# Linear attention and a top-1 mixture of experts on one core: decay tables made in place, counts, slots and fetches moved, the last stores deferred

## The chip, the cores and the metric

The kernel runs on one core of a Trainium2 chip. The metric is the device time of one execution in microseconds (us). Matmuls run on TensorE (PE), elementwise work on VectorE (DVE), ScalarE (ACT) and GpSimd (POOL). DMAs are issued from the queues of SyncE (SP), of ACT and of POOL; POOL issues the indirect ones, which gather or scatter rows by an index. Each engine works through its instructions in the order in which they stand, and an instruction that waits holds up all that stand behind it on that engine.

## What is computed

The reference has two parts. The first is linear attention with a decay per head, for 4 batches, 8 heads, 768 positions and 64 features, written here by blocks of 64 positions:

```python
Dmask = np.where(rel >= 0, lam ** rel, 0.0)             # rel = i - j, per head
intra = ((qb @ kb.T) * Dmask) @ vb
inter = (qb * lam ** (pos + 1)) @ kv_state
out[block] = intra + inter
kb_dec = kb * lam ** (block - 1 - pos)
kv_state = lam ** block * kv_state + kb_dec.T @ vb
```

Its output is read as 3072 tokens of 512 features, `x`. The second part sends each token to one of 8 experts:

```python
logits = x @ w_gate + modality_bias[modality_id]
e_idx = argmax(logits)
gate_w = softmax(logits)[e_idx]
h = relu(x[e_idx == e] @ w1[e])                          # w1: 512 x 1024
out[e_idx == e] = gate_w * (h @ w2[e])                   # w2: 1024 x 512
```

## The kernel before

**Attention.** The 24 chunks of 128 positions are worked on in 12 pairs `j`, with one load of 2 MB a pair (`load_half`, L190, three buffers): keys and queries with features in the partitions, values and keys with positions there. For a chunk PE computes scores (L232), DVE multiplies them by the decay table `dk` into `pt` (`masked`, L239), and PE multiplies `pt` by the values (`outputs`, L285) and adds the queries times the state (`from_state`, L278). DVE scales the queries by the table `pq` (`queries`, L222) and the keys by `kdec`, a copy of columns of `dk` (`keys`, L212); PE makes keys times values (`key_values`, L252), and the state is faded on POOL (L265) and added to on DVE (`carried`, L263 and L267). ACT copies the outputs to `xt`, PE turns them into token rows together with the gate's logits (`tokens`, L296), ACT copies these to `xn` (L298) and stores them to the DRAM tensor `xs`.

**The tables.** `lam` is loaded to 8 partitions, its powers are built by seven doublings on DVE (L83) into `tab`, stored to DRAM (`tab_d`, L86) and read back by two DMAs in overlapping rows as `dk` (L90). `pq` comes from PE, by matmuls of the powers with a selecting matrix (`spread_powers`, L109). Until work can begin, PE runs `keep_busy` (L806), matmuls of a tile of zeros.

**Routing.** After the last pair of a batch, `gates`, `route`, `ranks` and `places` (L305 to L382) find for each token its expert and its place among that expert's tokens, and `write_slots` scatters the token's number and weight to `inv` in DRAM (L389, POOL, one indirect DMA for a chunk). `count_tiles` (PE L406, DVE L408 to L413) counts the tokens of each expert up to then. Count "A" is made before the attention ends and gives the two early tiles; count "B" comes from all tokens and gives the list of the others.

**Experts.** A tile has 256 tokens of one expert. The indices of its rows are fetched (SP, L578), the rows gathered into `xg` (POOL, L588), and turned by PE in two parts of four matmuls (`turn_part`, L623), here called T0 and T1. Each fp32 operand is split into a rounded part and a rest (ACT L553, DVE L554), and each product is made of three matmuls (`three`, L636, L639, L640). `wide` makes the first product in four groups, after each of which ACT and DVE make `hh` and `hl` and run a `tail`: it splits a quarter of w2. In the first tile the tails also carry work of the routing of the last batch (`first_tail`): the second one finishes places, the third one writes slots and makes count "B". `second` makes the second product in two halves `t` of 128 tokens, ACT scales it into `y` (L728), and POOL scatters the rows to the output (`store`, L712). The weights of later tiles are fetched by SP.

**The end.** How many tiles there are depends on the data. A fixed number runs always; the rest are nested branches on a count (L1053), none of which is entered in the profiled execution. The second half of the last fixed tile is scaled into a part of `dk`, which is free by then (L725), and its scatter, `store_rest` (L1065), is issued behind the branches.

**Order.** `pinned` chains instructions in the order in which the code makes them, engine by engine; `behind` adds an order, with or without a wait, between two instructions. What is not chained is placed by a scheduler.

Of the kernel before, what the change touches and what calls it, by code (L numbers as in the profile page):

```python
# [6 lines left out]
F32 = mybir.dt.float32  # L7
# [12 lines left out]
HB = 2  # L20
# [20 lines left out]
def linear_attention_moe(tc, qkv, lam, modality, wg, mbias, w1, w2, out):  # L41
    nc = tc.nc
    with ExitStack() as ctx:
# [17 lines left out]
        lam8 = const.tile([H, 1], F32, name="lam8")  # L61
        nc.sync.dma_start(out=lam8, in_=lam)
# [9 lines left out]
        for c in range(HB):  # L72
            for part in (slice(0, 2), slice(2, 4)):
# [3 lines left out]
        tab = const.tile([H, 2 * P], F32, name="tab")  # L77
        nc.vector.memset(tab[:, 0 : P - 1], 0.0)
        nc.vector.memset(tab[:, P - 1 : P], 1.0)
        pw = tab[:, P - 1 :]  # L80
        nc.vector.tensor_copy(out=pw[:, 1:2], in_=lam8)
        for n in (1, 2, 4, 8, 16, 32, 64):
            powers = nc.vector.tensor_scalar(out=pw[:, n + 1 : 2 * n + 1], in0=pw[:, 1 : n + 1],  # L83
                                             scalar1=pw[:, n : n + 1], scalar2=None, op0=ALU.mult)
        tab_d = dram.tile([H, 2 * P], F32, name="tab_d")
        nc.scalar.dma_start(out=tab_d, in_=tab)  # L86

        dk = const.tile([P, 2, NP, P], F32, name="dk")
        for hl in range(2):
            tables = nc.sync.dma_start(  # L90
                out=dk[:, hl],
                in_=bass.AP(tensor=tab_d.tensor, offset=tab_d.offset + hl * 2 * P,
                            ap=[[1, P], [4 * P, NP], [1, P]]),
            )
# [4 lines left out]
        which = const.tile([H, NP, 2, D], F32, name="which")  # L99
        nc.gpsimd.memset(which, 0.0)  # L100
        nc.gpsimd.affine_select(out=which, in_=which, pattern=[[-2, NP], [-1, 2], [0, D]], compare_op=ALU.not_equal,
                                fill=1.0, base=0, channel_multiplier=1)

        pq = const.tile([P, NP, P], F32, name="pq")

        def spread_powers():
            pp = ps.tile([P, NP, P], F32, name="x", bufs=1)
            for p in range(NP):
                nc.tensor.matmul(pp[:, p, :], which[:, p].rearrange("h a d -> h (a d)"), pw[:, 1 : P + 1],  # L109
                                 start=True, stop=True)  # L110
            nc.scalar.copy(out=pq, in_=pp)
# [1003 lines left out]
```

## Time and profile before

| | us |
|---|---|
| median of 3 runs | 417.57 |
| lowest and highest | 417.11, 418.16 |
| the profiled execution | 416.55 |
| its span in the profile | 414.7 |

The granted clock of TensorE was 0.992 over the span. The profile gives, for one execution, the busy time of each engine, what ended each engine's idle time, and a timeline of the instructions. Times within it count from the start of the span. The page shows PE busy in nearly all of the 40 slices of the span; DVE and ACT are idle for a good part, and POOL for most. A matmul of filler counts as busy like any other.

### The profile page before, as it was taken

The numbers are of one execution on the slowest core, as the hardware profiler recorded it, in microseconds if no ns is written. First come the engines' busy times: TensorE is split into PE (matmuls) and PEld (weight loads), VectorE is DVE, ScalarE is ACT, GpSimd is POOL, SyncE is SP. The second block draws the span as 40 slices with busy tenths as digits, with TensorE's granted clock in tenths as the row PEclk, the third lists the DMA queues.
The fourth block names the chain that finished last, engine by engine and source line by source line (L and its number), as shares of the span: only waits on it lengthen the run. The fifth ranks groups of instructions, "written<-read, shape, count | busy, mean of one in ns | idle before, by whom it ended". The sixth has DMA issues, their size and how long they took to land.

```text
span 414.7 us, 9616 instructions
## 1 busy us (share of the span) xinstructions
PE 396.6 (96%) x3864; PEld 353.9 (85%) x3864; DVE 252.1 (61%) x435; ACT 181.2 (44%) x273; POOL 110.0 (27%) x117
## 2 busy tenths in 40 slices
PE   8899999999988999999999999999999999999990
PEld 4599999898886987788989999898989899898980
DVE  5678777879869850667482837466483837375510
ACT  1123323324546331466473726365463827364410
POOL 5010144164156511213031222203040222202000
PEclk9999999999999999999999999999999999999996
DMA  6999999995910176012026584402011111100000
GB/s 210 332 391 381 389 368 337 352 377 216 332 71 3 61 270 242 19 49 81 25 73 235 199 303 143 151 27 80 27 55 51 55 51 38 59 2 28 27 28 19
DMA packets 23347, 63.81 MB, mean 154 GB/s; under 512 B 6901, under 2 KB 8445, under 8 KB 21248
## 3 DMA queue, kind: packets, MB, share of 16 engines
q1 hardware_dynamic: 15056, 43.36, 28.8%
q0 software_dynamic: 4768, 13.08, 9.5%
q10 hardware_dynamic: 3472, 6.69, 4.2%
q8 instruction: 32, 0.52, 0.5%
q14 instruction: 19, 0.16, 0.1%
HBM read 91.40 MB, written 14.07 MB: 254 GB/s over the span
## 4 chain that ended last, share of the span: by engine, by line
PE 42%; issue 29%; DMA 13%; POOL 6%; DVE 3%; another core or an unknown queue 2%; ACT 2%; SPq 1%; POOLq 1%; DVEq 0%; ACTq 0%
DMA out_dram<-y,idx 7%; PE s L232 6%; PE x L296 5%; PE o L285 5%; POOL out_dram L712 4%; PE o L278 3%; DMA idx<-inv 3%; PE s L636 3%; PE s L640 3%; PE s L639 3%; PE o L636 3%; PE o L640 3%; PE o L639 3%; POOL xg L588 2%; PE kv L252 2%
## 5 line engine op out<-in xcount | busy, mean ns | idle before, releaser
L636 PE MATMUL s<-xh,w1h 128*128 128x256 f32 x384 | 108.2, 282 | 1.3 <-DVE hl L654 1.0
L640 PE MATMUL s<-xh,w1l 128*128 128x256 f32 x384 | 107.8, 281 | 0.0
L639 PE MATMUL s<-xl,w1h 128*128 128x256 f32 x384 | 107.8, 281 | 0.0
L654 DVE SCALAR_TENSOR_TENSOR hl<-s,hh 128x512 fp32r<-128x512 f32 x48 | 33.2, 691 | 85.9 <-ACT hh L653 84.2
L636 PE MATMUL o<-w2h,hh 128*128 128x512 f32 x192 | 75.8, 395 | 0.0
L636 PEld LDWEIGHTS s<-xh,w1h 128*128 128x128 f32 x384 | 72.1, 188 | 3.3 <-issue 1.8
L640 PE MATMUL o<-w2h,hl 128*128 128x512 f32 x192 | 74.8, 390 | 0.0
L639 PE MATMUL o<-w2l,hh 128*128 128x512 f32 x192 | 74.8, 389 | 0.0
L640 PEld LDWEIGHTS s<-xh,w1l 128*128 128x128 f32 x384 | 73.5, 191 | 0.0
L639 PEld LDWEIGHTS s<-xl,w1h 128*128 128x128 f32 x384 | 72.2, 188 | 0.4
L554 DVE TENSOR_TENSOR w2l<-raw,w2h 128x1024 fp32r<-128x1024 f32 x48 | 58.8, 1224 | 10.9 <-ACT w2h L553 10.7
L653 ACT ACTIVATE hh<-s 128x512 fp32r<-128x512 f32 x48 | 28.7, 599 | 71.4 <-PE s L640 60.3
L554 DVE TENSOR_TENSOR w1l<-raw,w1h 128x1024 fp32r<-128x1024 f32 x46 | 53.5, 1218 | 4.5 <-ACT yn L700 3.3
L712 POOL DMA_INDIRECT out_dram<-y,idx x19 | 27.4, 1445 | 93.4 <-ACT y L728 93.4
L553 ACT CAST w2h<-raw 128x1024 fp32r<-128x1024 f32 x48 | 49.9, 1039 | 0.0
L588 POOL DMA_INDIRECT xg<-xs,idx x20 | 23.1, 1156 | 85.5 <-PE kv L623 80.9
L553 ACT CAST w1h<-raw 128x1024 fp32r<-128x1024 f32 x46 | 45.2, 1064 | 0.0
L640 PEld LDWEIGHTS o<-w2h,hl 128*128 128x128 f32 x192 | 36.0, 188 | 7.6
L639 PEld LDWEIGHTS o<-w2l,hh 128*128 128x128 f32 x192 | 36.1, 188 | 7.2
L636 PEld LDWEIGHTS o<-w2h,hh 128*128 128x128 f32 x192 | 36.1, 188 | 7.2
L389 POOL DMA_INDIRECT inv<-pay,sloti x24 | 29.5, 1231 | 27.0 <-PE x L296 6.6
L298 ACT COPY xn<-x 128x272 f32<-128x272 f32 x42 | 16.3, 388 | 46.2 <-PE x L296 46.2
(215 smaller groups left out, 470.6 us busy)
## 6 DMA issues: line engine op xcount, KB each, us to landing
raw<-in_w_dram SPq DMA_DIRECT2D x52, 1024.0 KB
load<-in_qkv_dram SPq DMA_DIRECT2D x11, 2048.0 KB
xs<-xn ACTq DMA_DIRECT2D x24, 272.0 KB
load<-in_qkv_dram SPq DMA_DIRECT2D x4, 512.0 KB
w2f<-in_w_dram SPq DMA_DIRECT2D x2, 1024.0 KB
w1h<-in_w_dram SPq DMA_DIRECT2D x2, 1024.0 KB
dk<-tab_d SPq DMA_DIRECT2D x2, 256.0 KB
inv<-pad SPq DMA_DIRECT2D x2, 196.0 KB
```

Of the source, the lines that this page charges most:

```text
L232: pinned(nc.tensor.matmul(sp[:, hl, p, :], kt[r, p, :], qt[r, p, :], start=True, stop=True))
L285: mm = pinned(nc.tensor.matmul(op[blk][halves2[hl ^ blk], p, :], vt[:, (2 * p + hl) * D : (2 * p + hl + 1) * D], pt[:, hl, p, :], start=(g ...
L389: sc = nc.gpsimd.indirect_dma_start(out=inv, out_offset=bass.IndirectOffsetOnAxis(ap=at, axis=0), in_=pay[:, c, :], in_offset=None)
L553: cp = nc.scalar.copy(out=hi, in_=src)
L554: df = nc.vector.tensor_tensor(out=lo, in0=src, in1=hi.bitcast(F32), op=ALU.subtract)
L588: last = nc.gpsimd.indirect_dma_start(out=(to or xg)[t][:m], out_offset=None, in_=xs[:rows, :], in_offset=bass.IndirectOffsetOnAxis(ap=idx ...
L636: mm = pinned(nc.tensor.matmul(out, ah, bh, start=first, stop=False))
L639: pinned(nc.tensor.matmul(out, ah, bl, start=False, stop=False))
L640: return pinned(nc.tensor.matmul(out, al, bh, start=False, stop=last))
L653: act = nc.scalar.activation(out=hh[i], in_=hp, func=AF.Relu)
L654: low = nc.vector.scalar_tensor_tensor(out=hl[i], in0=hp, scalar=0.0, in1=hh[i].bitcast(F32), op0=ALU.max, op1=ALU.subtract)
L712: sc = nc.gpsimd.indirect_dma_start(out=out, out_offset=bass.IndirectOffsetOnAxis(ap=idx[:, t, 0:1], axis=0), in_=y, in_offset=None, bound ...
```

## The change

**Tables.** `lam` is loaded as one row, by ACT's queue. PE multiplies a row of ones by it, which puts the eight decays into each of 128 partitions; DVE copies them, and makes the tables by twelve running products (`tensor_tensor_scan`, 128x128 each): eight for `dk`, each of which starts at the partition's diagonal by a one from `anti`, and four for `pq`. The doublings, `tab_d` and `which` are gone. The filler is 4, 8, 2 and 4 matmuls instead of 16 and 20, with the spreading, scores(0) and scores(1) between.

**Loads.** The quarters of the first load come by part, then by chunk; the second load comes in four pieces with the gate's weights between, the third in two. No load stands behind the tables any more.

**The first two pairs.** Keys and queries are scaled by chunk, the first queries on POOL; the state's first copy is on ACT, and matmuls and DVE work are in another order. Several constants are made by POOL rather than DVE.

**Slots, indices, w2.** At pair `early + 1` one more slot is written, and the index fetches for the early tiles are moved there from the pair behind it. The fetch of w2 waits for the row gather to land; before it waited for a small memset on POOL that stood behind the gather's issue.

**After the attention** the turns T0 and T1 of the first tile stand between the tokens groups of the last chunks, and one `xn` copy of the last chunk goes from DVE to ACT. **Count "B"** goes from the third tail of the first tile to the fourth. **At the end** both halves of the last fixed tile are scaled into `dk`, and `store_rest` issues both scatters.

```diff
+        def spread_decays():
+
+            lp = ps.tile([P, 2, NP], F32, name="x", bufs=1)
+            pinned(nc.tensor.matmul(lp.rearrange("p h a -> p (h a)"), row, lam1, start=True, stop=True))
+            pinned(nc.vector.tensor_copy(out=lamb, in_=lp))
+            for hl in range(2):
+                for p in range(NP):
+                    pinned(nc.vector.tensor_tensor_scan(
+                        out=dk[:, hl, p, :], data0=lamb[:, hl, p : p + 1].to_broadcast([P, P]),
+                        data1=anti, initial=0.0, op0=ALU.mult, op1=ALU.add))
+            for hl, r in enumerate(halves2):
+                pinned(nc.vector.tensor_copy(out=lamp[r], in_=lamb[r, hl]))
+            for p in range(NP):
+                powers.append(pinned(nc.vector.tensor_tensor_scan(
+                    out=pq[:, p, :], data0=lamp[:, p : p + 1].to_broadcast([P, P]),
+                    data1=zero, initial=1.0, op0=ALU.mult, op1=ALU.add)))
...
-        keep_busy(16)
-        sp = scores(0)
-        spread_powers()
-        keep_busy(20)
+        list_constants()
+        keep_busy(4)
+        spread_decays()
+        keep_busy(8)
+        sps = [scores(0)]
+        keep_busy(2)
+        sps.append(scores(1))
+        keep_busy(4)
...
-        pt = masked(0, sp)
-        kds[0] = keys(0)
-        qds[0] = queries(0)
+        pts = [masked(0, sps[0])]
+        kds[0] = keys(0, c0)
+        pts.append(masked(1, sps[1]))
+        qds[0] = queries(0, c1, eng=nc.gpsimd)
...
+            if j == 1:
+                qds[1] = queries(1, c0)
+                pts = [masked(gs[0], sps[0])]
+                kds[1] = keys(1, c0)
+                pts.append(masked(gs[1], sps[1]))
+                queries(1, c1, qds[1])
+                next(turns)
+                next(turns)
+                kp, _ = key_values(gs[:1])
+                carried(gs[0], kp)
+                keys(1, c1, kds[1])
...
+            if j == early + 1:
+                write_slot(mm)
...
-            elif j == early + 2:
+            elif j == early + 1:
                 for i in range(EARLY):
                     fetch_idx(listA, i, idxA[i], after=loads[-1])
+            elif j == early + 2:
                 gathered = fetch_rows(idxA[0], TT, SOON * S, after=fades[-1])
-                asked = nc.gpsimd.memset(flag, 0)
-                behind(asked, gathered, wait=False)
-                fetch_w2(er, {}, asked)
+                fetch_w2(er, {}, gathered)
         turns = turned(pairs - 1)
+        next(turns)
+        rows0 = turn_part(0, TT, pin=True)
+        next(turns)
+        split(*rows0)
+        rows1 = turn_part(1, TT, pin=True)
+        split(*rows1)
         next(turns)
         next(turns)
         gated(pairs - 2)
-        rows0 = turn_part(0, TT, pin=True)
-        split(*rows0)
-        rows1 = turn_part(1, TT, pin=True)
-        next(turns)
-        split(*rows1)
-        next(turns)
...
             elif i == 2:
                 write_slots(next(begun[1]), begun[0])
+            else:
                 begun.append(count_tiles(XT + 1, "B"))
...
-                if kept is not None and t == 1:
-                    nc.scalar.activation(out=kept, in_=yp, func=AF.Copy, scale=weight)
-                    return lambda: store(kept, 1)
+                if kept is not None:
+                    nc.scalar.activation(out=kept[t], in_=yp, func=AF.Copy, scale=weight)
+                    continue
...
+            return lambda: [store(kept[t], t) for t in range(2)]
...
-        kept = dk[:, 0].rearrange("p a t -> p (a t)")
+        kept = [dk[:, t].rearrange("p a t -> p (a t)") for t in range(2)]
```

Three places show what this makes of the order of instructions. DVE at the start, before, from the doublings on (x2 means twice in a row):

```order
L83 TENSOR_SCALAR tab<-tab 8x16
L83 TENSOR_SCALAR tab<-tab 8x32
L83 TENSOR_SCALAR tab<-tab 8x64
L410 TENSOR_SCALAR geA<-thr 1x96
L410 TENSOR_SCALAR geB<-thr 1x96
L239 TENSOR_TENSOR pt<-s,dk 128x512 x2
L212 TENSOR_TENSOR kd<-load,kdec 128x1024
L222 TENSOR_TENSOR qd<-load,pq 128x512
L263 COPY state_117<-kv 128x256
L239 TENSOR_TENSOR pt<-s,dk 128x1024
L212 TENSOR_TENSOR kd<-load,kdec 128x1024
L222 TENSOR_TENSOR qd<-load,pq 128x1024
```

And after; the running products are shown under the name of their kind, at L85 and L91:

```order
L151 MEMSET onesb 128x128
L82 COPY lamb<-x 128x8
L85 SCALAR_TENSOR_TENSOR dk<-lamb,anti 128x128 x8
L89 COPY lamp<-lamb 64x4 x2
L91 SCALAR_TENSOR_TENSOR pq<-lamp,zero 128x128 x4
L242 TENSOR_TENSOR pt<-s,dk 128x512 x2
L213 TENSOR_TENSOR kd<-load,kdec 128x512
L242 TENSOR_TENSOR pt<-s,dk 128x1024
L213 TENSOR_TENSOR kd<-load,kdec 128x512
L270 TENSOR_TENSOR state_108<-faded,kv 128x256
L225 TENSOR_TENSOR qd<-load,pq 128x512
L242 TENSOR_TENSOR pt<-s,dk 128x1024
```

The two operations on `geA` and `geB` and the doublings are gone from there, twelve running products stand ahead of the first `pt`, and a half `kd`, the second `pt` and the other half follow, where the whole `kd` and a `qd` stood.

PE around count "B" in the first tile, before, between the third and the fourth group of the first product (`s`):

```order
L636 MATMUL s<-xh_135,w1h 128x256
L639 MATMUL s<-xl_137,w1h 128x256
L640 MATMUL s<-xh_135,w1l 128x256
L406 LDWEIGHTS onesb
L406 MATMUL kv<-ohsum,onesb 128x8
L636 MATMUL s<-xh_134,w1h 128x256
L639 MATMUL s<-xl_136,w1h 128x256
L640 MATMUL s<-xh_134,w1l 128x256
```

And after, at the end of the fourth group:

```order
L639 MATMUL s<-xh_121,w1h 128x256
L642 MATMUL s<-xl_123,w1h 128x256
L643 MATMUL s<-xh_121,w1l 128x256
L409 LDWEIGHTS onesb
L409 MATMUL kv<-ohsum,onesb 128x8
L626 MATMUL x<-ident,xg_116 128x128
L626 MATMUL x<-ident,xg_117 128x128
L626 MATMUL x<-ident,xg_116 128x128
L626 MATMUL x<-ident,xg_117 128x128
L639 MATMUL o<-w2h,hh_1802 128x512
L642 MATMUL o<-w2l,hh_1802 128x512
L643 MATMUL o<-w2h,hl_1804 128x512
```

The count's matmul now stands one group of 24 matmuls later, right ahead of T0 (the turns into `x`); T1 (the turns into `kv`) comes behind the first twelve matmuls of the second product, where it stood right behind T0.

POOL ahead of the first branch, before:

```order
L588 DMA xg_126<-xs,idx_4397 128x544
L588 DMA xg_127<-xs,idx_4397 128x544
L712 DMA out_dram<-y,idx_3927 3072x512 x2
L712 DMA out_dram<-y,idx_4162 3072x512 x2
L712 DMA out_dram<-y,idx_4397 3072x512
L1053 COMPARE_AND_BRANCH
L588 DMA xg_126<-xs,idx_4923 128x544
```

The same after:

```order
L591 DMA xg_116<-xs,idx_4386 128x544
L591 DMA xg_117<-xs,idx_4386 128x544
L715 DMA out_dram<-y,idx_3916 3072x512 x2
L715 DMA out_dram<-y,idx_4151 3072x512 x2
L715 DMA out_dram<-dk,idx_4386 3072x512
L1078 COMPARE_AND_BRANCH
L591 DMA xg_116<-xs,idx_4908 128x544
```

And after, the end of POOL's instructions:

```order
L1078 UNCONDITIONAL_BRANCH
L1078 ISA
L1078 UNCONDITIONAL_BRANCH
L715 DMA out_dram<-dk,idx_4386 3072x512
L1136 UNCONDITIONAL_BRANCH
L1136 ISA
```

One scatter from `y` became one from `dk` in the same place ahead of the branch, and one scatter from `dk` stands behind the branches, as one did before.

## Rows read from the trace of the kernel before

**Rows 1.** The page, busy time of TensorE: us, share of the span, instructions.

```profile
PE 396.6 (96%) x3864; PEld 353.9 (85%) x3864; DVE 252.1 (61%) x435; ACT 181.2 (44%) x273; POOL 110.0 (27%) x117
```

**Rows 2.** Waits of PE: engine, line, waited for: us, times, longest.

```profile
PE kv L623 <- DVE cntB L408: 2.0, 1, 2.0
PE kv L252 <- DVE kd L212: 1.8, 1, 1.8
...
PE kv L406 <- DVE ohsum L376: 1.0, 1, 1.0
```

**Rows 3.** Timeline of PE, 0 to 31: start, us, engine, line, operation [idle before].

```profile
1.28 5.55 PE L806 MATMUL o<-busy 128*128 128x512 bf16 x16 [1.28 <-DVE busy L76]
...
9.91 3.63 PE L806 MATMUL o<-busy 128*128 128x512 bf16 x16
15.38 0.69 PE L252 MATMUL kv<-load,kd 128*64 128x64 f32 x16 [1.84 <-DVE kd L212]
...
17.09 1.09 PE L285 MATMUL o<-pt,load 128*64 128x128 f32 x16
...
28.79 2.06 PE L232 MATMUL s<-load 64*128 64x128 f32 x32
```

**Rows 4.** Timeline of DVE, 0 to 16.

```profile
3.02 0.08 DVE L81 COPY tab<-lam 8x1 f32<-8x1 f32 x1
...
6.08 1.07 DVE L410 TENSOR_SCALAR geA<-thr 1x96 f32<-1x96 f32 x1 [0.35 <-POOL thr L789]
...
12.83 1.36 DVE L239 TENSOR_TENSOR pt<-s,dk 128x512 f32<-128x512 f32 x2 [5.63 <-DMA dk<-tab_d]
14.11 1.22 DVE L212 TENSOR_TENSOR kd<-load,kdec 128x1024 f32<-128x1024 f32 x1
15.24 0.68 DVE L222 TENSOR_TENSOR qd<-load,pq 128x512 f32<-128x512 f32 x1
```

**Rows 5.** DVE groups by shape, 0 to 60: busy us, mean ns of one.

```profile
L267 DVE TENSOR_TENSOR state<-faded,kv 128x256 f32<-128x256 f32 x8 | 3.4, 421 | 5.6 <-POOL faded L265 2.9 <-PE kv L252 2.6
L222 DVE TENSOR_TENSOR qd<-load,pq 128x512 f32<-128x512 f32 x3 | 2.1, 684 | 0.0
```

**Rows 6.** POOL groups by shape, 0 to 30.

```profile
L265 POOL TENSOR_TENSOR faded<-state,pq 128x256 f32<-128x256 f32 x4 | 2.5, 623 | 16.6 <-DVE state L267 10.5 <-DVE state L263 6.1
L139 POOL COPY iw<-ident 64x256 f32<-64x256 f32 x4 | 1.6, 396 | 0.2
L137 POOL MEMSET iw<- 128x544 f32 x2 | 1.2, 593 | 0.0
```

**Rows 7.** Stretches: us, busy of PE, PEld, DVE, ACT, POOL, PEclk, DMA share, GB/s.

```profile
3.00:5.00 2.00, 2.00 (x6) 0.71 (x5) 1.63 (x15) 0.00 (x0) 0.00 (x0) 1.00 1.03 360
...
9.00:10.00 1.00, 1.00 (x9) 0.88 (x9) 0.00 (x0) 0.00 (x0) 0.93 (x5) 1.00 0.02 5
10.00:13.00 3.00, 3.00 (x15) 1.35 (x15) 0.17 (x1) 0.59 (x1) 0.55 (x3) 1.00 0.80 193
...
20.00:28.00 8.00, 8.00 (x184) 7.64 (x179) 6.22 (x8) 2.86 (x7) 1.25 (x2) 1.00 1.02 411
```

**Rows 8.** Timeline of DVE, 118 to 130.

```profile
120.39 0.17 DVE L376 TENSOR_TENSOR ohsum<-ohsum,ohn 128x8 bf16<-128x8 bf16 x1
123.33 0.69 DVE L654 SCALAR_TENSOR_TENSOR hl<-s,hh 128x512 fp32r<-128x512 f32 x1 [2.78 <-ACT hh L653]
...
125.96 0.11 DVE L408 COPY cntB<-kv 1x8 f32<-1x8 f32 x1
126.10 0.24 DVE L411 TENSOR_TENSOR geB<-cntB,geB 1x96 f32<-1x96 f32 x1
```

**Rows 9.** Timeline of ACT, 118 to 130.

```profile
122.70 0.60 ACT L653 ACTIVATE hh<-s 128x512 fp32r<-128x512 f32 x1 [4.38 <-remote]
```

**Rows 10.** Timeline of POOL, 380 to 415.

```profile
406.59 0.98 POOL L712 DMA_INDIRECT out_dram<-dk,idx  x1 [5.34 <-DMA out_dram<-y,idx]
```

**Rows 11.** Timeline of ACT, 398 to 415.

```profile
404.69 0.69 ACT L725 ACTIVATE dk<-o,idx 128x512 f32<-128x512 f32 x1 [4.70 <-PE o L640]
```

More of the change, by code (lines that the diff above doesn't have):

```diff
@@ L58, in behind, with pinned @@
             tc.add_manual_dep(later.ins, first.ins.name, info, reason="order")
-        lam8 = const.tile([H, 1], F32, name="lam8")
-        nc.sync.dma_start(out=lam8, in_=lam)
+        halves2 = [slice(hl * D, (hl + 1) * D) for hl in range(2)]
+        pins = {}
+        def pinned(op):
+            if op.ins.engine in pins:
+                behind(op, pins[op.ins.engine], wait=False)
+            pins[op.ins.engine] = op
+            return op
+        lam1 = const.tile([1, H], F32, name="lam1")
+        nc.scalar.dma_start(out=lam1, in_=lam)
+        row = const.tile([1, P], F32, name="row")
+        nc.vector.memset(row, 1.0)
+        lamb = const.tile([P, 2, NP], F32, name="lamb")
+        lamp = const.tile([P, NP], F32, name="lamp")
+        def spread_decays():
[13 more added lines that the diff above has]
+                    data1=zero, initial=1.0, op0=ALU.mult, op1=ALU.add)))
         def load_tile():
@@ L71, in linear_attention_moe @@
         first = load_tile()
-        for c in range(HB):
-            for part in (slice(0, 2), slice(2, 4)):
+        for part in (slice(0, 2), slice(2, 4)):
+            for c in range(HB):
                 nc.sync.dma_start(out=first[:, part, c], in_=source(0)[:, part, c])
@@ L76, in linear_attention_moe @@
         nc.vector.memset(busy, 0.0)
[L77 to L86, printed above, removed]
-        dk = const.tile([P, 2, NP, P], F32, name="dk")
[L89 to L94, printed above, removed]
+        zero = const.tile([P, P], F32, name="zero")
+        nc.vector.memset(zero, 0.0)
+        anti = const.tile([P, P], F32, name="anti")
+        nc.gpsimd.affine_select(out=anti, in_=zero, pattern=[[1, P]], compare_op=ALU.not_equal,
+                                fill=1.0, base=1 - P, channel_multiplier=1)
+        dk = const.tile([P, 2, NP, P], F32, name="dk")
+        pq = const.tile([P, NP, P], F32, name="pq")
+        powers = []
         ident = const.tile([P, P], F32, name="ident")
@@ L98, in linear_attention_moe @@
         wgt = const.tile([P, HB, NP, E], F32, name="wgt")
[L99 to L111, printed above, removed]
         def later(op):
-            behind(op, powers)
+            behind(op, powers[-1])
             return op
@@ L189, in load_half @@
             t = load_tile()
-            ld = nc.sync.dma_start(out=t, in_=source(g))
-            behind(ld, tables, wait=False)
+            whole = slice(0, HB)
+            for part in (slice(0, 2), slice(2, 4)) if g < LOADS else (slice(0, 4),):
+                for c in (slice(i, i + 1) for i in range(HB)) if g == 1 else (whole,):
+                    ld = nc.sync.dma_start(out=t[:, part, c], in_=source(g)[:, part, c])
+                    if g == 1 and part.start == c.start == 0:
+                        nc.sync.dma_start(out=wgt, in_=wg)
             loads.append(ld)
@@ L262, in carried @@
             if c == 0:
-                return pinned(nc.vector.tensor_copy(out=new, in_=kp[:, g % HB]))
+                return pinned(copy(out=new, in_=kp[:, g % HB]))
             faded = work.tile([P, NP, D], F32, name="faded", bufs=1)
@@ L601, in fetch_regs, with fetch_halves @@
             return er, {"cond": cr}
-        def fetch_halves(to, src, er, kw, after):
+        def fetch_halves(to, src, er, kw, after, wait):
             n = src.shape[2] // 2
```

141 lines of the change are left out of this document (69 added, 72 removed).

## Prediction

> **What bounds the kernel now.** I read the page's busy times first. TensorE (PE) is busy in 396.6 us of the 414.7 us span [rows 1], so time can be won in two ways alone: by taking out waits of PE, or by letting it reach its first useful matmul sooner. The list of PE's waits [rows 2] has three that this change could touch: 2.0 us before the second half of a turn (L623), which waits for VectorE's (DVE's) copy of a count, 1.8 us at the start before the first key-value products, and 1.0 us before the count's matmul (L406).
>
> PE's own rows at the start [rows 3] say more than its waits. From 1.28 to 13.54 us it does filler (L806 on a tile of zeros: 16 in the first row, 16 in the last), one scores group and the spreading of the powers; only at 15.38 does kv (L252) begin, and from there PE works without a pause to the scores at 28.79. The filler counts as busy, so the loss is not the 1.8 us of the list but most of 15 us. DVE's rows [rows 4] name what it waits for: lam's copy starts at 3.02, the powers are built and sent to DRAM and back, and the masked scores start at 12.83 after 5.63 us idle, ended by the table's DMA. Then pt takes 1.28 us to the start of kd at 14.11, and kd ends at 15.33, 0.05 before kv.
>
> **The start, A.** Tables no longer go through DRAM: PE spreads the eight decays, DVE copies them and makes twelve running products of 128x128, and pt, half of kd and kv follow. lam now comes by the ACT queue; I keep its time, 3.0. The small matmul and DVE's copy bring the first product to about 3.6. The trace before has no such running product, so I bound one by other DVE rows [rows 5]: 128x256 takes 0.421 and 128x512 takes 0.684, which is 0.158 plus 1.03 ns a column, and a follower starts some 0.09 before the end shown (kd to qd in [rows 4]: 14.11 + 1.22 against 15.24). For 128 columns at that rate the spacing is 0.20. Since every product needs the one before it, I take two column times for an element, 0.42 less 0.09, or 0.33; as a high bound 0.50, three column times. So the tables are done at 3.6 + 12 x 0.33 + 0.3 for the two small copies = 7.9 (6.3 to 9.9). Add 1.28 for pt and 0.69 for one half of kd: kv at K = 9.9.
>
> [...]
>
> PE itself can't be there much sooner: from 1.28, four fillers, the spreading, eight, scores(0), two, scores(1), four. With 0.35 for one of the early fillers (5.55 / 16), 0.23 for a late one (3.63 / 16) and 1.03 for each scores group (2.06 / 2) [rows 3], that is 1.28 + 12 x 0.35 + 0.2 + 1.03 + 0.5 + 1.03 + 0.9 = 9.1. So faster products can bring up to 0.8 more. The first loads are ahead of this: at 360 GB/s [rows 7], 2 MB take about 5.8 us, and the quarter that kd needs is the third.
>
> From kv on, before takes 13.41 us to the scores at 28.79. After has 1.0 less, since scores(1) stands ahead of kv, but DVE becomes the bound once: from_state(1) needs the second state of the pair, behind pt(2), pt(3), one half of kd and two of qd. PE reaches kv(1)'s end at K + 4.2 (kv 0.6, outputs, from_state, outputs 1.0 each [rows 3], kv 0.6); DVE then does a state, two halves of kd or qd before pt(3), two pt, one half after and the state: 2 x 0.42 + 3 x 0.6 + 2 x 1.13 = 4.9, plus a 0.4 wait for the first scores: K + 9.6. PE wants it at about K + 8.7. With 0.4 for two tokens groups in a row that share one PSUM tile, the scores come at K + 12.4 + 1.4 = K + 13.8 to 14.1. I take K + 14.1 = 24.0, so A gains **4.8**.
>
> Does it last? Between 9 and 10 us DMA moves 5 GB/s and from 10 to 13 it moves small pieces of the table at less than half of the later rate [rows 7]; without them the loads begin about 5 us sooner. So loads and PE shift by nearly the same amount, and I let the gain hold. The qd that goes to POOL, 128x512, is hidden: twice the 0.62 of a 128x256 there [rows 6], from the tables' end to about 9.2, and PE wants it 1.7 after K.
>
> **The early tiles, B.** The 1.0 us at L406 goes wholly: the count now stands behind the last wide group, 24 matmuls later, and ohsum was ready at 120.56 [rows 8]. The 2.0 us wait hides a queue on DVE: hl at 123.33 came late because ACT's hh began at 122.70 after 4.38 us idle [rows 9], and the count's copy stood behind it, w2l and three small operations, at 125.96 [rows 8]. After, T0 and twelve matmuls of the second product (12 x 0.23 = 2.7 us) stand between the count and T1, but the copy stands behind hl and w2l of the last quarter too (0.69 [rows 8] and, as other operations of 128x1024, 1.22 [rows 4]). I expect 0.0 to 1.3 us of it to remain and take 0.4, so 1.6 is won. Of the turns that are now spread between the last tokens groups I count nothing: one xn copy goes to ACT, which is busy with casts there. B gains 1.0 + 1.6 = **2.6**, between 1.0 and 3.0. The list that follows the count starts behind the same w1l casts as before, so nothing later moves.
>
> **Slots, index fetches and w2.** The added write_slot and the index fetch one pair sooner lie on POOL and SP while PE works; w2's fetch now waits for the landing of the row gather rather than its issue. SP has no load queued behind it, and w2 is not used until the first second product. Counted at 0, up to 1 us lost if it lands late.
>
> **The tail, D.** POOL's last scatter starts at 406.59 although ACT's tile was ready at 404.69 + 0.69 = 405.38 [rows 10, 11]: its idle time ended on the landing of the scatter before it, for which the branch's bookkeeping on POOL waits. With both scatters behind the branches that bookkeeping would be over long before, and the last scatter would start 1.1 us sooner. But the order of the changed program has one scatter of dk ahead of the first branch and one behind, as before. I follow the order: **0**.
>
> **Sum.** 4.8 + 2.6 + 0 = 7.4. The profiled execution took 416.55 (414.7 of span, 1.85 around it) and would take 409.2; it lies 1.0 under the median, 417.57, so the forecast is 417.57 - 7.4 = **410.2**.
>
> **Rivals.** (1) The scatters do go behind the branches, as the change says: 409.1. For it, the source; against it, the order. (2) T1 still waits for the count and the start is as forecast: gain 4.8 + 1.0, 411.8. For it, ACT's late hh [rows 9]. (3) The products are slowed by POOL, which builds iw and the list constants at the same time. Before, a DVE operation of 1x96 took 1.07 at 6.08 [rows 4], where one of that shape takes 0.24 later [rows 8]; POOL filled iw and the list constants then. Three POOL copies of 0.4 [rows 6] beside the products make the tables 1.2 later: A is 3.6, the time 411.4. [...] (4) Slower: a running product costs an element what the slow 1x96 row cost, 11 ns [rows 4], so 1.43 each. Tables at 3.6 + 17.2 + 0.3 = 21.1, K at 23.1, scores at 37.2, 8.4 lost against 2.6 won: 423.4. It decides from 0.95 us each on, where A loses what B wins. Against it, the rows of full tiles cost 1.3 to 1.6 ns a column [rows 5].
>
> **How the numbers follow.** Forecast 0.52, (1) 0.10, (2) 0.13, (3) 0.14, (4) 0.04; 0.07 for smaller losses that add up (A at 2, B at 1: 414.6). The range leaves out (4) and the worst of the last: 407.8 (A 5.6, B 3.0, D 1.1) to 413.6. A difference within 0.3% (1.25 us) can't be told from none. Faster by more 0.93, within 0.03, slower 0.04.
>
> **What would show it.** A: dk's products end near 7.9 and kv starts near 9.9; a spacing of 0.2 or 0.5 is read at once from DVE's rows, and a new PE wait of about 1 us before the second half of from_state(1). B: no wait at L409, and under 1.3 before T1. D: POOL's last scatter again about 1.2 us after ACT's tile. I am wrong if PE reaches the scores of the third pair later than 26, or if a gain there is back by 100 us as waits for loads.

## The result, and the profile after

The changed kernel took 413.2 us in the median (412.57 to 416.87, 12 runs) against 418.32 for the kernel before in the same comparison (414.77 to 421.35, 12 runs): a ratio of 0.9893, with a 95% interval of 0.9860 to 0.9926. On the 417.57 us that the prediction starts from that is a gain of 4.5 us (3.1 to 5.8 by the interval), where 7.4 was forecast; 413.1 lies inside the range, 0.5 from its slow end. The profiled execution's span is 411.2 us where before had 414.7. Some executions of a kernel are slower as a whole; the ratios leave these out and are not made from the medians, so they need not be the quotients of the medians beside them.

TensorE's waits in the changed kernel (engine, line, what it waited for: us, times, longest):

```profile
PE o L815 <- DVE busy L107: 1.4, 1, 1.4
PE x L299 <- ACT xn L301: 1.1, 2, 0.6
PE s L639 <- DVE hl L657: 0.8, 1, 0.8
PE kv L255 <- DVE kd L213: 0.7, 1, 0.7
PE o L281 <- DVE state L270: 0.5, 1, 0.5
```

The two waits of 2.0 and 1.0 us around the count [rows 2] are gone, and the start's 1.8 is 0.7. A wait for `hl` in the third expert tile is left as it was, 0.8 at 174 us here and 1.0 at 180 us before:

```profile
PE s L636 <- DVE hl L654: 1.0, 1, 1.0
```

TensorE's rows at the start (start, us, operation, idle before it):

```profile
10.67 0.69 PE L255 MATMUL kv<-load,kd 128*64 128x64 f32 x16 [0.74 <-DVE kd L213]
...
17.82 0.68 PE L299 MATMUL x<-iw,xt 128*64 128x136 f32 x8 [0.49 <-ACT xn L301]
...
19.82 1.09 PE L281 MATMUL o<-qd,state 64*64 64x128 f32 x28 [0.48 <-DVE state L270]
...
24.60 2.06 PE L235 MATMUL s<-load 64*128 64x128 f32 x32
```

`kv` begins at 10.67 instead of 15.38 and the scores of the third pair at 24.60 instead of 28.79 [rows 3], 4.19 us sooner. VectorE's rows of the same stretch, where the tables are made:

```profile
3.86 0.17 DVE L82 COPY lamb<-x 128x8 f32<-128x8 f32 x1 [0.48 <-PE x L81]
4.13 2.94 DVE L85 TENSOR_TENSOR_SCAN dk<-lamb,anti 128x128 f32<-128x128 f32 x8
6.99 0.31 DVE L89 COPY lamp<-lamb 64x4 f32<-64x4 f32 x2
7.34 1.37 DVE L91 TENSOR_TENSOR_SCAN pq<-lamp,zero 128x128 f32<-128x128 f32 x4
8.63 1.26 DVE L242 TENSOR_TENSOR pt<-s,dk 128x512 f32<-128x512 f32 x2
9.81 0.81 DVE L213 TENSOR_TENSOR kd<-load,kdec 128x512 f32<-128x512 f32 x1
```

Eight running products take 2.94 us, 0.367 each in the mean, and four take 1.37, 0.34 each. The loads no longer stop for the table [rows 7] (stretch: busy of PE, PEld, DVE, ACT, POOL, clock, DMA share, GB/s):

```profile
9.00:10.00 1.00, 0.88 (x3) 0.20 (x3) 1.00 (x3) 0.00 (x0) 1.00 (x1) 1.00 1.04 366
10.00:13.00 3.00, 2.33 (x48) 2.16 (x48) 2.35 (x3) 0.96 (x2) 2.54 (x7) 1.00 1.05 389
```

Behind the attention VectorE copies the count (L411) at 122.02 in the changed kernel, and no row of TensorE waits for it:

```profile
116.89 0.17 DVE L379 TENSOR_TENSOR ohsum<-ohsum,ohn 128x8 bf16<-128x8 bf16 x1
...
122.02 0.15 DVE L411 COPY cntB<-kv 1x8 f32<-1x8 f32 x1
```

So far all is near the forecast. Set side by side, the two profiled executions show where the gain stood: the changed kernel is ahead by 4.19 us at the third pair's scores, by 3.41 at the first matmul of the first expert tile (110.64 and 107.23), by 6.53 at that of the second tile (137.55 and 131.02), and by 3.89 at the last tile's second product (393.61 and 389.72). **2.64 us are lost over eleven tiles in which TensorE waits in neither kernel but for that one `hl` of the third, 1.0 before and 0.8 after.** One first product of each, from its first matmul to the turn behind its 96th, is enough to see it. Before (the start is the first number):

```profile
220.57 0.28 PE L636 MATMUL s<-xh,w1h 128*128 128x256 f32 x1
...
231.88 0.60 PE L623 MATMUL x<-ident,xg 128*128 128x128 f32 x4
```

After:

```profile
215.01 0.28 PE L639 MATMUL s<-xh,w1h 128*128 128x256 f32 x1
...
226.54 0.60 PE L626 MATMUL x<-ident,xg 128*128 128x128 f32 x4
```

11.31 us before, 11.53 after, for the same 96 matmuls of the same shape at a full clock (1.00 granted): 0.1178 and 0.1201 us apart, 0.22 a tile, 2.4 of the 2.64 in eleven tiles; most of the rest is in the third tile. The matmuls of the second product are 0.227 apart in both.

### The profile page after: what moved, and what is told of

The parts are those of the page before. It is cut to its first block, busy times and chain, and to the rows that moved or that the text cites. A ratio compares the mean times of both kernels' runs of the same rounds, so it can differ in the third digit from the quotient of the medians.

```text
span 411.2 us, 9569 instructions
## 1 busy us (share of the span) xinstructions
PE 395.3 (96%) x3839; PEld 354.5 (86%) x3840; DVE 252.4 (61%) x438; ACT 181.6 (44%) x274; POOL 113.6 (28%) x119
## 4 chain that ended last, share of the span: by engine, by line
PE 61%; issue 21%; DMA 7%; POOL 5%; DVE 3%; another core or an unknown queue 1%; ACT 1%; POOLq 1%; DVEq 0%; ACTq 0%
DMA out_dram<-y,idx 7%; PE s L639 6%; PE s L642 6%; PE s L643 6%; PE o L288 5%; PE o L639 5%; PE o L643 5%; PE o L642 5%; PE x L299 5%; PE s L235 5%; PE o L281 3%; POOL out_dram L715 3%; PE kv L255 2%; POOL xg L591 2%; PE s L674 1%
## 5 line engine op out<-in xcount | busy, mean ns | idle before, releaser
L591 POOL DMA_INDIRECT xg<-xs,idx x20 | 24.0, 1202 | 87.0 <-PE kv L626 82.8
L715 POOL DMA_INDIRECT out_dram<-y,idx x18 | 26.2, 1457 | 78.1 <-ACT y L731 74.7
L392 POOL DMA_INDIRECT inv<-pay,sloti x24 | 28.5, 1189 | 22.3 <-PE x L299 8.1
```

The source lines that it names most:

```text
L392: sc = nc.gpsimd.indirect_dma_start(out=inv, out_offset=bass.IndirectOffsetOnAxis(ap=at, axis=0), in_=pay[:, c, :], in_offset=None)
L591: last = nc.gpsimd.indirect_dma_start(out=(to or xg)[t][:m], out_offset=None, in_=xs[:rows, :], in_offset=bass.IndirectOffsetOnAxis(ap=idx ...
L715: sc = nc.gpsimd.indirect_dma_start(out=out, out_offset=bass.IndirectOffsetOnAxis(ap=idx[:, t, 0:1], axis=0), in_=y, in_offset=None, bound ...
```

## The experiments

Each ratio is against runs of the kernel before on the same chip, which differ from chip to chip by some 7 us (medians of 413.3 to 420.6); I compare the times of one chip with each other. "Changed kernel" is after, "a32" is the changed kernel with the edit of the first experiment.

### What makes the same matmuls slower: the place in SBUF

The diff does not touch the first product. What it changes for it is where the tiles lie: other constants are placed ahead of them. `strip` is a small constant that is placed between the tokens `xh`, `xl` and the weights `w1h`, `w1l`; a wider `strip` moves the weights and all behind it, not the tokens. `row` is placed ahead of both. The first four kernels, on one chip (before 414.0 us), are the changed kernel again, two that move its tiles, and before with the move of a32:

```diff
 a32: the changed kernel, weights 32 bytes further
-        strip = const.tile([P, 2], F32, name="strip")
+        strip = const.tile([P, 16], F32, name="strip")
 a64: the changed kernel, tokens and weights 64 bytes further
-        row = const.tile([1, P], F32, name="row")
+        row = const.tile([1, P + 16], F32, name="row")[:, :P]
 b32: the kernel before, weights 32 bytes further
-        strip = const.tile([P, 2], F32, name="strip")
+        strip = const.tile([P, 16], F32, name="strip")
```

> The changed kernel once more, beside the others on one chip. Every theory: span near 411.2, time 1.1% below before; matmuls of the first product of a tile 0.1201 us apart.

> The changed kernel with one small constant tile (strip) made 32 bytes wider a partition, so that all that lies behind it, w1h and w1l among it, starts at a multiple of 64 bytes as before; no instruction differs. Theory 1 (the first product runs slower since its weights lie 32 bytes past a multiple of 64): the spacing falls from 0.1201 to 0.1178, 0.21 us a tile, 2.3 to 2.7 us in all, span 408.5 to 408.9. Theory 2 (xh and xl, 64 bytes past a multiple of 128, are to blame) and theory 3 (it is not the place in memory but what runs beside it): 411.2 as the changed kernel.

> The changed kernel with an early constant tile (row) made 64 bytes wider, so that xh and xl start at a multiple of 128 as before, and w1h and w1l stay 32 bytes past a multiple of 64; no instruction differs. Theory 2: spacing 0.1178, span near 408.7. Theories 1 and 3: 0.1201 and 411.2.

> The kernel before with strip 32 bytes wider, so that w1h and w1l lie 32 bytes past a multiple of 64; xh and xl stay where they were; no instruction differs. Theory 1: it loses what the changed kernel lost, spacing 0.1201, 2.3 to 2.7 us, span 417.0 to 417.4. Theories 2 and 3: 414.7 as before.

The changed kernel again took 410.56 us (ratio 0.9919 [0.9889, 0.9949]), a32 408.04 (0.9851 [0.9818, 0.9884]), a64 410.54 (0.9909 [0.9875, 0.9942]), b32 416.46 (1.0059 [1.0032, 1.0086]). 32 bytes in a constant that has nothing to do with the product bring 2.5 us, and the first product of a32 is back at 11.31 us. Moving both operands alike brings nothing, so it is not the place of one that counts. The wider `strip` makes the kernel before slower: the sign depends on where one starts. None of the three theories on record holds as it stands: theory 1 wanted 0.1201 us between the matmuls of b32, which has 0.1187; a64 speaks against theory 2 and a32 against theory 3. b32's 2.5 us are more than its first products explain (11.39 for 11.31, 1.0 us in twelve tiles); the rest stays open.

Two larger moves have one run each, and the third and fourth run repeat a move beside a32 (before 413.32 us):

```diff
 a_s64: the changed kernel, weights 64 bytes further
+        strip = const.tile([P, 24], F32, name="strip")
 b96: the kernel before, weights 96 bytes further
+        strip = const.tile([P, 32], F32, name="strip")
```

> The changed kernel with strip 64 bytes wider: w1h and w1l still lie 32 bytes past a multiple of 64, but 64 bytes further from xh. Counted modulo 128, w1h less xh was 32 in the two kernels with the full loss (0.1201 us apart, 0.21 us a tile) and 96 in the one of before with shifted weights (0.1187, 0.09 a tile). If that distance sets the size: 0.1187 here. If the program does, or the weights' place alone: 0.1201 as in the changed kernel.

> The kernel before with strip 96 bytes wider: w1h and w1l lie 32 bytes past a multiple of 64, and w1h less xh is 32 modulo 128. If the distance sets the size of the loss: 0.1201 and 0.21 us a tile. If the program does: 0.1187 and 0.09 a tile as with strip 32 bytes wider.

> The changed kernel with strip 64 bytes wider, timed beside a32 on one chip. In its first trace the matmuls of the first product stood 0.1167 us apart, closer than in the kernel before (0.1178). If that holds: 1152 x 1.1 ns = 1.3 us below a32. If it was that execution's: as a32 or above.

> a32 as the yardstick: 1.3 to 1.5% below before, spacing 0.1178.

a_s64 took 410.82 us and b96 421.03 beside a single 417.12 of before; a_s64_again 407.83 (0.9849 [0.9805, 0.9893]), a32_third 407.87 (0.9854 [0.9810, 0.9898]). A first product takes 11.21 us in a_s64, the least of all, and 11.52 in b96. The distance modulo 128 had given b96 rightly and a_s64 wrongly (0.1187 expected, 0.1168 measured). What orders them is the distance from the tokens to the weights modulo 256 bytes, which I found only after these seven placements. The last run was to forecast an eighth: before with 160 bytes more has the distance 224 of a_s64.

```diff
 b160: the kernel before, weights 160 bytes further
+        strip = const.tile([P, 48], F32, name="strip")
```

> The kernel before with its small tile strip made 48 columns wide, so that everything placed behind it in SBUF, the first product's weights among it, lies 160 bytes further while the tokens stay. Theory (the distance from the tokens to the weights, taken modulo 256, sets the spacing of the first product's matmuls): the distance goes from 64 to 224, which was the fastest with the changed kernel; the matmuls start 0.1167 us apart where before has 0.1178, 0.11 us less per tile of 96, about 1.2 us less over the program. Rival (each shift of the weights of before costs, as 32 bytes did with 0.1187 and 96 bytes with 0.1201): 0.120 or more, the program some 2.5 us longer than before.

Its first product:

```profile
198.79 0.28 PE L636 MATMUL s<-xh,w1h 128*128 128x256 f32 x1
...
210.00 0.60 PE L623 MATMUL x<-ident,xg 128*128 128x128 f32 x4
```

11.21 us, as a_s64 has, to the hundredth; the rival's 11.5 is out. The time was 418.36 us against 420.55 on that chip (0.9972 [0.9936, 1.0009]), which agrees with the 1.2 us forecast and can't by itself be told from none. All eight (bytes within a partition, from the compiled programs):

| kernel | weights at | tokens at | distance mod 256 | one first product, us |
|---|---|---|---|---|
| before | 146496 | 81408 | 64 | 11.31 |
| b32 | 146528 | 81408 | 96 | 11.39 |
| b96 | 146592 | 81408 | 160 | 11.52 |
| b160 | 146656 | 81408 | 224 | 11.21 |
| changed | 145376 | 79936 | 160 | 11.53 |
| a32 | 145408 | 79936 | 192 | 11.31 |
| a_s64 | 145440 | 79936 | 224 | 11.21 |
| a64 | 145440 | 80000 | 160 | 11.52 |

a64 and a_s64 have their weights in one place and differ by 0.31 us; changed and a_s64 share the tokens' place and differ by 0.32. The other twelve traces, at distances of 64, 160, 192 and 224, have the same times to 0.01. That the distance sets it is inferred from these eight, of which one was forecast. All that lies behind `strip` moves with the weights, so that it is the weights and not another tile there is argued, from what the product reads; why the distance matters is not shown. The times follow less exactly than the traces: a_s64_again should be 1.2 us below a32_third and is 0.04 below, with a wait of 1.0 for a row gather in its profiled execution.

### What the start is worth

a32scan2 is a32 with the four products of `pq` made twice, so that `kv` begins later and nothing else changes. a32order is a32 with the order that the kernel before has for the first two pairs, tables and loads as changed. Since a32order was on another chip, a32 was run again beside it, and a64order is the same edit on a_s64.

```diff
 a32scan2
+            for p in range(NP):
+                powers.append(pinned(nc.vector.tensor_tensor_scan(
+                    out=pq[:, p, :], data0=lamp[:, p : p + 1].to_broadcast([P, P]),
+                    data1=zero, initial=1.0, op0=ALU.mult, op1=ALU.add)))
 a32order
-        pts = [masked(0, sps[0])]
-        kds[0] = keys(0, c0)
-        pts.append(masked(1, sps[1]))
-        qds[0] = queries(0, c1, eng=nc.gpsimd)
+        pt = masked(0, sp)
+        kds[0] = keys(0)
+        qds[0] = queries(0)
...
-            if j == 1:
-                qds[1] = queries(1, c0)
-                pts = [masked(gs[0], sps[0])]
-                kds[1] = keys(1, c0)
...
+            pts = [masked(g, sp) for g, sp in zip(gs, sps)]
```

> a32 with the four running products of pq made twice, 1.37 us more of DVE's work ahead of pt. If the chain of products sets the start (A as forecast): kv 1.3 later, at 12.0, and the time 1.2 to 1.4 us above a32, so near 409.3. Rival, the loads set the pace after the first pairs and the start has slack: within 0.4 us of a32.

> a32 with the work of the first two pairs in the order of the kernel before (whole kd, first qd and state on DVE, scores(1) behind kv, one more filler), tables and loads as changed. If the tables are what A is worth: kv at 11.2 rather than 10.7, no waits at tokens and from_state(1) (0.5 each in a32), the scores of the third pair within 0.3 us of a32's 24.6 and the time within 0.4 us. If the order by chunk carries a part of A: scores of the third pair at 25.5 or later and 0.8 to 1.5 us above a32.

> a32 once more, as the yardstick of the three kernels beside it. If its gain is the forecast's A and B without the loss to the place of the weights: 1.3 to 1.8% below before.

> a_s64 with the first two pairs in the order of the kernel before (as a32order, which took a32's time): within 0.3 us of a_s64, 0.1167 apart.

a32scan2's scores of the third pair come at 25.88, 1.28 later than 24.60, and its time is 411.97 us (0.9865 [0.9807, 0.9923]); the nearest kernel on that chip, a32tact below, took 410.73. So a delay of the start comes out at the end, 1.24 of 1.28 if a32tact stands for a32, though an interval of 2 us to each side does not prove the size. The two traces say the same: what is 1.28 later at the third pair is 1.12 later at the first matmul of the last tile (377.15 and 376.03). a32order took 408.3 us (0.9870 [0.9839, 0.9901]), a32_again 408.27 (0.9868 [0.9836, 0.9899]), a64order 407.57 (0.9865 [0.9806, 0.9923]) beside 407.83 of a_s64_again. TensorE's rows of a32order:

```profile
11.11 0.69 PE L255 MATMUL kv<-load,kd 128*64 128x64 f32 x16 [1.65 <-DVE kd L213]
...
24.52 2.06 PE L235 MATMUL s<-load 64*128 64x128 f32 x32
```

`kv` begins 0.44 later and the third pair no later: the whole of the start comes from tables and loads, which no run separates, and the work by chunk in the first pairs is worth nothing.

### The count

```diff
 bcnt: the kernel before, count "B" in the fourth tail
             elif i == 2:
                 write_slots(next(begun[1]), begun[0])
+            else:
                 begun.append(count_tiles(XT + 1, "B"))
 a32cnt: a32, count "B" back in the third tail
-            else:
```

> The kernel before with one part of the change alone: count B in the fourth tail of the first tile instead of the third; memory as before. As forecast for B: 1.0 us at the count's matmul and 1.6 before T1, time 2.6 us or 0.6% below before. If the wait before T1 is not there in most executions: 0.7 to 1.0 us, 0.2%. Rival, the count's copy behind hl and w2l makes T1 wait in its place: no gain.

> a32 with count B back in the third tail. As forecast for B: 1.0 us at the count's matmul and up to 2.0 before T1 come back, time 1.0 to 3.0 us above a32. Rival, the count was hidden in most executions: within 0.4 us of a32.

bcnt took 417.22 us beside 419.17 of before, 0.9989 [0.9951, 1.0027]: not to be told from none. Both waits at the count are gone from its trace, and a new one stands in the first product of the second tile:

```profile
PE s L636 <- DVE hl L654: 1.9, 2, 1.0
```

Before has 1.0 there in one wait, bcnt 1.9 in two: near 1 us of the 3 is given back. The changed kernel has no such wait in its second tile. a32cnt took 409.52 (0.9894 [0.9863, 0.9926]), 1.25 more than a32_again on its chip:

```profile
PE kv L409 <- DVE ohsum L379: 0.7, 1, 0.7
```

The wait of 0.7 at the count's matmul is back; that before T1 is not. T1's wait is no fixed price in the kernel before either: 2.0, 2.1, 2.0 and 1.3 us in the profiled executions of before, b_again, b160 and b96, and none in that of b32. Where it is 2.0 or 2.1, ACT's `hh` comes late, behind an idle time that ends on something the profile does not name (`remote`), as in [rows 9]; here in b_again, with 4.43 in b160 and no such row in b32:

```profile
126.81 0.60 ACT L653 ACTIVATE hh<-s 128x512 fp32r<-128x512 f32 x1 [4.39 <-remote]
```

It seems to go by the chip. The nine traces that have the wait for `hl` in the third tile, of 0.7 to 1.0, come from the first comparison and from chips where before takes 417 to 421 us, and T1's wait is in all four of them that count in the third tail. The other eleven, b32 and a32cnt among them, are from chips where before takes 413.3 to 414.4, and have neither. What ACT waits for stays open.

### The slot

a32slot is a32 without the additional `write_slot` at pair `early + 1`.

```diff
-            if j == early + 1:
-                write_slot(mm)
```

> a32 without the one added slot write at pair early + 1 (it moves into the next slot's place, all slots are still written). If that write costs PE a wait at 80 to 86 us (0.5 to 0.6 in the changed kernel, after ACT's xn or a state): the wait is gone, 0.4 to 0.6 us below a32. If the wait comes from elsewhere: within 0.3 us of a32, or up to 0.5 above where the index fetch then waits for the slots.

It took 409.2 us (0.9889 [0.9848, 0.9931]), 0.9 more than a32_again; the intervals overlap. The wait of 0.5 near 81 us that it was to remove is still there, and its trace has a wait that a32 has not: T0 waits for the gathered rows.

```profile
PE x L626 <- DMA xg<-xs,idxA: 0.5, 1, 0.5
```

a_s64_again, which writes the additional slot, waits there too, for 1.0, so that this wait comes from the slot is not shown.

### The tail

The changed order has one of the two scatters of `dk` ahead of the first branch. a32tact lets the first wait for ACT's last scaling, so that both stand behind the branches.

```diff
+            def rest():
+                first = store(kept[0], 0)
+                behind(first, scaled[1], wait=True)
+                store(kept[1], 1)
```

> a32 with the scatter of the first half made to wait for ACT's last scaling, by which both scatters come to stand behind the branches. If the branch's bookkeeping behind the early scatter sets the last one's start: it is off the path, but two scatters must now be issued from 0.2 us after ACT's end, 1.27 apart, so the last starts 1.4 to 1.5 after ACT's end where it was 1.5 in the changed kernel: time within 0.3 us of a32. If scatters close behind each other also land later: 0.3 to 1 us above a32.

It took 410.73 us (0.9819 [0.9766, 0.9873]). POOL's last rows, and ACT's last scaling:

```profile
399.42 0.98 POOL L715 DMA_INDIRECT out_dram<-dk,idx  x1 [21.19 <-ACTq L1085]
400.70 0.99 POOL L715 DMA_INDIRECT out_dram<-dk,idx  x1 [0.30 <-issue]
```

```profile
398.46 0.69 ACT L730 ACTIVATE dk<-o,idx 128x512 f32<-128x512 f32 x1 [4.75 <-PE o L643]
```

The last scatter starts 1.55 us after ACT's end (399.15 to 400.70). In the changed kernel, where it waits for the scatter before it, it is 1.54 (401.54 to 403.08), in a32 1.40, and 1.33 to 1.95 over the thirteen traces of that order:

```profile
396.37 0.98 POOL L715 DMA_INDIRECT out_dram<-dk,idx  x1 [15.98 <-ACT dk L728]
403.08 0.98 POOL L715 DMA_INDIRECT out_dram<-dk,idx  x1 [5.72 <-DMA out_dram<-y,idx]
```

```profile
400.85 0.69 ACT L728 ACTIVATE dk<-o,idx 128x512 f32<-128x512 f32 x1 [4.75 <-PE o L643]
```

No a32 was timed beside a32tact, so what its time gained is not shown. In its trace the wait on the early scatter's landing is only traded for the scatter ahead, 1.28 long. A first scatter behind the branches that does not wait for the last scaling was not tried.

### The kernel before, once more

Before varies by 4 to 7 us between executions on one chip, the changed kernel by 2 to 4. A second trace of it shows one possible reason:

> The kernel before once more, for a second trace of it. If the 2.0 us wait ahead of T1 in the first trace belongs to the program, it is here again. If it comes from one late release (ACT's hh began 3.1 us after its matmuls had ended there), it is gone or shorter here, and B was worth 1.0 us rather than 2.6 in most executions.

It took 420.68 us. The table's second DMA landed late there, and VectorE's second `pt` waited for it; the wait for `kd` is 3.2 us instead of 1.8, and behind it TensorE's granted clock, the third number from the end in the stretches, is half:

```profile
15.10 0.69 DVE L239 TENSOR_TENSOR pt<-s,dk 128x512 f32<-128x512 f32 x1 [0.74 <-DMA dk<-tab_d]
```

```profile
PE kv L252 <- DVE kd L212: 3.2, 1, 3.2
```

```profile
16.00:18.00 2.00, 1.02 (x16) 0.93 (x16) 1.53 (x2) 0.00 (x0) 0.00 (x0) 0.50 1.01 418
18.00:20.00 2.00, 2.00 (x18) 1.79 (x16) 0.42 (x1) 0.00 (x0) 0.62 (x1) 0.50 1.04 317
20.00:22.00 2.00, 2.00 (x20) 1.63 (x18) 1.84 (x2) 0.00 (x0) 0.00 (x0) 0.50 0.92 365
22.00:24.00 2.00, 2.00 (x30) 1.83 (x30) 1.06 (x2) 0.58 (x1) 0.00 (x0) 0.81 1.00 406
```

Ahead of `kv`, which runs at 0.50 and takes 1.12 us where it took 0.69 [rows 3], TensorE had no matmul for 3.22 us; in the first trace the pause there is 1.84 us and the clock behind it stays at 1.00 (16 to 20 us). That the longer pause halves the clock is not shown by this one trace. The scores of the third pair come at 32.99, 4.2 after those of [rows 3]. None of the fourteen traces with the new tables has such a stretch. How often it happened in the timed runs is not shown, but their mean granted clocks point that way: it is 0.983 in b_again, at most 0.985 in 13 of the 111 timed executions of before and its variants in these experiments, this one among them, and at least 0.986 in all 68 of the changed kernel and its variants.

## Why the prediction was right or wrong

**The start, A: right, a little too large.** 4.8 was forecast, and the third pair's scores came 4.2 sooner, at 24.60 for 24.0. The first product began at 4.13 instead of 3.6, twelve of them took 4.3 us instead of 4.0, so `kv` came at 10.67 for 9.9; from there 13.93 us for 14.1. The two pauses that I foresaw as 0.4, a guess that no row gives, and about 1 were 0.49 and 0.48. That a running product takes two column times, 0.33, was my estimate, which no row of the kernel before shows; it held: they start 0.36 and 0.32 apart, against the 0.20 that [rows 5] give for 128 columns of the operations there. The price of rival 4 (1.43 each) is out. The high bound of 0.50, called three column times, is 0.46 by the rows that it names; it did not matter.

**Does it last? Mostly.** The lead of the changed kernel stays at 4.2 to 4.5 us up to 84 us. In the profiled execution 0.8 of it is lost around 86, most of it where TensorE waits for an `xn` copy of ACT's; a32scan2 and a32tact show that wait too, nine other runs of this order don't. On the chip of a_again and b32 nothing is lost: a_again is 4.37 us ahead at the third pair (24.59 and 28.96) and 4.60 at the first expert tile (105.41 and 110.01).

```profile
85.71 0.68 PE L299 MATMUL x<-iw,xt 128*64 128x136 f32 x8 [0.63 <-ACT xn L301]
```

**The count, B: the mechanism right, the size not one number.** Both waits went, as forecast, and of the 0.4 that I kept for T1 nothing came; rival 2 is out. In the profiled pair the stretch from the first to the second tile gained 3.1 us, more than the 2.6 forecast. But the price was read from one execution of before. Undone on another chip, the count's move is worth 1.25 us between medians, of which the trace has 0.7: T1's 2.0 is no fixed wait, and was not there. In bcnt a part of what is taken away comes back at an `hl` of the second tile.

**Slots: open.** They were counted at 0, up to 1 lost; a32slot's median says 0.9 won, inside the intervals, and of that its trace has 0.5, in a wait that comes and goes.

**The tail, D: right.** 0 was forecast from the order, and the last scatter starts 1.54 us after ACT's tile where [rows 10, 11] have 1.21, a third of a microsecond lost in this pair; over all twenty traces the figure goes from 1.21 to 1.95. Rival 1 promised 1.1 more if both went behind the branches; a32tact puts them there, and its last scatter starts no sooner after the tile.

**The step that failed** is "so nothing later moves". It was said of the list behind the count, but by it the sum took every matmul that the diff leaves alone as lasting what it lasted before. No instruction of the first product moved, but its operands did, and 96 matmuls take 11.53 us in place of 11.31: a term of +2.5 us (0.21 x 12 tiles) that the sum lacks. It is shown by a32, which removes it with a constant that the product doesn't read, and by a64, which moves both operands alike and removes nothing. That the time lies inside the range is no merit of the sum: the range was made wide for losses in A and B, and this term is not among them.

With it the account closes. In the two profiled executions of the first comparison the lead goes as follows, beside what the sum had:

| stretch | forecast, us | measured, us |
|---|---|---|
| to the third pair's scores | 4.8 | 4.19 |
| from there to the first expert tile | 0 | -0.78 |
| to the second tile (the count) | 2.6 | 3.12 |
| to the last tile's second product | 0 | -2.64 |
| to the last scatter | 0 | -0.38 |
| together | 7.4 | 3.51 |

The spans differ by 3.5, the times by the 4.5 of the ratio; before varies by more than that difference from one execution to the next. The largest single miss is the fourth line. With the weights moved, the median of a32_again is 6.1 us below that of before beside it (414.35 to 408.27): A 4.2 in the traces, the count 1.25, the slot up to 0.9, together 5.5 to 6.4, differences of medians that are each uncertain by some tenths. The changed kernel lacks 2.5 of that, and gains 3.4 (414.0 to 410.56) where a32 stood beside it.

**A better version** than both follows: the changed kernel with `strip` 16 or 24 columns wide, 407.8 to 408.3 us on chips where before takes 413.3 to 414.4, 1.3 to 1.5% below it.

## What to carry to other kernels

A wait that is read from one execution may have its size in that execution, or on that chip, alone, as T1's of 2.0, 2.1, 2.0, 1.3 us and none in five traces: take a second one before it goes into a sum. When a change adds or removes constants, compare the spacing of matmuls that it doesn't touch before anything else, since other tiles can then lie elsewhere: here the weights went from 146496 to 145376, the tokens from 81408 to 79936, and the spacing from 0.1178 to 0.1201 us. Shifting one tile by a few dozen bytes is a cheap test of it: 32 bytes brought 2.5 us in a32. Here a table made by running products where it is used beat one that goes through DRAM: the twelve products took 4.3 us, and `kv` began at 10.67 instead of 15.38. No load stands behind the table any more, and what that alone brings was not tested. A group's mean can hide a few slow instructions: that of the first eight products below is 0.43 us, of which two take 0.57 and 0.55 and six 0.39.

## What the hardware showed that was not expected

- The pace of the first product's matmuls, 256 columns each, went with where their two operands lie: 0.1168, 0.1178, 0.1187 or 0.1201 us between two, over distances of 224, 64 and 192, 96, and 160 bytes modulo 256. The second product, 512 columns, has 0.227 in each, but its operands (`w2h` and `hh`) lie 81920 bytes apart in all eight programs, so it says nothing on this.
- In the pairs below VectorE and POOL both read SBUF, and the one that started second took longer. A `faded` of 128x256 takes 1.00 us when it starts 0.17 behind a VectorE `qd` from two inputs in SBUF (the second row: 0.16 behind a `kd`, 19.68), where it took 0.62 [rows 6], and that `qd` has 0.69, where 0.68 is the mean before [rows 5]:

```profile
15.37 1.00 POOL L268 TENSOR_TENSOR faded<-state,pq 128x256 f32<-128x256 f32 x1 [2.54 <-DVE state L270]
19.84 1.00 POOL L268 TENSOR_TENSOR faded<-state,pq 128x256 f32<-128x256 f32 x1 [3.48 <-DVE state L270]
```

```profile
15.20 0.69 DVE L225 TENSOR_TENSOR qd<-load,pq 128x512 f32<-128x512 f32 x1
```

  The other way round it was VectorE that took longer. In a32 a `kd` of 128x512 starts while a `faded` is at work (19.85 to 20.85) and takes 1.08, where it takes 0.68 by itself; the `kd` at 9.81 above, 0.81, starts while POOL does its `qd`:

```profile
20.32 1.08 DVE L213 TENSOR_TENSOR kd<-load,kdec 128x512 f32<-128x512 f32 x1
```

  So too with the running products. The first two, which meet POOL's copies of `iw`, take 0.57 and 0.55, and the other ten 0.39 to 0.42 (least, median and most of the first eight, in ns, then POOL's row):

```profile
L85 DVE TENSOR_TENSOR_SCAN dk<-lamb,anti x8: 390/392/569, 4.1 to 6.7; 128x128 f32<-128x128 f32 x8
```

```profile
4.03 0.87 POOL L147 COPY iw<-ident 64x256 f32<-64x256 f32 x2
```

  Rival 3 was right in kind and too large: it put the tables 1.2 later, and these two products are 0.3 longer. What the two engines contend for is not shown.
